# Two small moves in a fused attention and GLU kernel: the loads of the output weights, and the norms of the fourth chunk

## The chip, the cores and the metric

The kernel runs on one core of one Trainium2 chip. A core has five engines with instruction streams of their own: TensorE (PE; matrix products), VectorE (DVE), ScalarE (ACT), GpSimd (POOL), and SyncE (SP), which here issues nearly all DMAs. The metric is device time in microseconds. The kernel before took 311.39 us, the median of three runs (310.5 to 311.7).

## The reference

One transformer block with its two branches side by side, B=1, S=2048 rows, D=640, bf16. Both branches read the same normalised rows.

```python
xn = layernorm(x)                       # over D, eps 1e-5
# A: attention, 32 heads of 20, causal, sliding window of 256 keys
q, k, v = split(xn @ wqkv)              # wqkv: 640 x 1920
p = softmax(where(0 <= i - j < 256, q @ k.T * 20**-0.5, -1e9))
a = (p @ v) @ wo                        # wo: 640 x 640
# B: gated GLU
b = (sigmoid(xn @ w_gate) * (xn @ w_up)) @ w_down   # F = 1536
out = x + a + b
```

## The kernel before, in words

**Chunks.** The 2048 rows are worked in four chunks (c = 0 to 3) of 512 rows, each of four blocks of 128 rows. For each chunk the kernel normalises the rows (`g_norms`), transposes them to `xnT[c]` (for c > 0 by a DMA transpose, `turn_block`), projects Q and K (`g_qk`: five blocks of Q, m = 0 to 4, then five of K, each five matmuls of 128x512), projects V (`g_v`), computes the 12 GLU products (`g_gu`: `pg`, then tanh on ACT, then `pu`, then `h` on DVE, L447), the attention in steps (`scores`, exponentials on ACT at L517, masks on POOL at L524 or as a minimum on DVE at L529, products with V in `pv`, whose sums are `acc`), and last the output (`g_out`: for each block of rows the down projection `y` over 12 `h` at L457, the output projection with `wo` at L464, the addition of x into `rows` at L468, the store at L479).

**Q and K through scratch memory.** A projected block is copied out of PSUM into one of six `st` buffers (Q by DVE at L323, K by ACT at L325) and stored to scratch in DRAM (L327, `sq` and `sk`); `spread` (L337) reads it back in the layout of the heads (`qT`, `kT`). An `st` buffer is free again when its store has landed. The Q gather of a chunk waits for all five Q stores.

**wo.** The rows of `wo` are reordered by `turn_wo` (eight DMAs from DRAM to DRAM, `wo_i`), then loaded into SBUF by `load_wo` (L237, four DMAs of 200 KB, 32 partitions each). In the program all four are issued at once, behind the fourth Q store of chunk 1 (`g_qk`, c = 1, m = 3); they are preceded on the queue by `wo_i`, five loads of `wd` and two stores that clear scratch.

**Order.** The order is written out by hand: each engine runs its instructions in the program's order. The main loop runs over the attention steps; between two steps a `Fill` object pulls dense work (projections, GLU, output) from a list of generators, a fixed amount per step, and each generator yields after a piece of matmuls. `mix(a, b, first, every)` runs generator a and, after its piece number `first` and then after each `every`-th, takes one step of b. So a generator like `g_norms` is a list of small steps, and an extra empty `yield 0` in it moves what follows behind one more piece of a.

**g_norms.** For each of the four row blocks: two `bn_stats` and a `bn_aggr` on DVE, one block per step. Then, after `behind` empty steps, `rstd_blocks` (two POOL instructions, L286 and L287), four empty steps, and the four normalisations `xn` on DVE (L292), one per step. With `turn` each is followed by its DMA transpose on SP (L303); for chunk 3 the transposes come from `g_turns(3)` after the norms. Chunk 3's norms are mixed first into `gu1b` (GLU products 7 to 11 of chunk 1, ten pieces, one norm step after each) and then, for what is left, into `out1`, after its piece 1 and every third piece from there. `out1` is chunk 1's output with the first GLU product of chunk 2 inside.

Of the kernel before, what the change touches and what calls it, by code (L numbers as in the profile page):

```python
# [20 lines left out]
HG = 4  # L21
# [91 lines left out]
def kernel(  # L113
# [11 lines left out]
    nc = tc.nc  # L125
# [30 lines left out]
    def load_x(c):  # L156
        t = xp.tile([P, SBC, D], BF16, name="xc")
        xc[c] = t
        nc.sync.dma_start(out=t, in_=xr[:, c * SBC:(c + 1) * SBC, :])
# [6 lines left out]
    wo = const.tile([P, DC, D], BF16, name="wo")  # L166
# [33 lines left out]
    def load_gu(t, w, k, lo=0, hi=FS):  # L200
        nc.sync.dma_start(out=t[k][:, :, lo:hi],
                          in_=w.rearrange("(c p) f -> p c f", p=P)[:, :, k * FS + lo:k * FS + hi])
# [24 lines left out]
    wo_i = tc.dram_tile([HG, NG * DH, D], BF16, name="wo_i")  # L227
# [4 lines left out]
                nc.sync.dma_start(out=wo_i[i].rearrange("(b a d) n -> a b d n", a=2, d=DH)[a],  # L232
                                  in_=A_wo.rearrange("(a b i d) n -> i a b d n", a=2, i=HG, d=DH)[i, a])

    def load_wo():
        for i in range(HG):
            nc.sync.dma_start(out=wo[32 * i:32 * i + 32, :, :],  # L237
                              in_=wo_i[i].rearrange("(m j) n -> j m n", j=32))


    ident = const.tile([P, P], BF16, name="ident")
# [39 lines left out]
    def ln_block(c, s, mv=None):  # L281
        return ln_mv(ln_half(c, s, 1, ln_half(c, s, 0)), mv)

    def rstd_blocks(mvs):
        rstds = lnp.tile([P, SBC], FP32, name="rstds", bufs=1)
        nc.gpsimd.tensor_scalar(out=rstds, in0=mvs[:, :, 1], scalar1=EPS, scalar2=None, op0=ADD)  # L286
        nc.gpsimd.tensor_tensor(out=rstds, in0=rstds, in1=neghalf, op=POW)  # L287
        return rstds

    def norm_block(c, s, mv, rstd):  # L290
        xn = lnp.tile([P, D], BF16, name="xn")
        nc.vector.tensor_scalar(out=xn, in0=xc[c][:, s, :], scalar1=mv[:, 0:1],  # L292
                                scalar2=rstd[:, 0:1], op0=SUB, op1=MULT)
        xns[c, s] = xn
# [7 lines left out]
    def turn_block(c, s):  # L302
        nc.sync.dma_start(out=xnT[c][:, :, s * P:(s + 1) * P], in_=xns.pop((c, s)), transpose=True)  # L303

    def new_xnT(c):
        xnT[c] = xtp.tile([P, DC, CW], BF16, name="xnT")
# [5 lines left out]
    def proj_block(w, c, m):  # L312


        base = 0 if w == "q" else D
        ps = ps_d.tile([P, CW], FP32, name="pqk", tag="d")
        for d in range(DC):
            wt = wqkv[:, d, base:base + D].rearrange("p (k m) -> p m k", m=DC)
            nc.tensor.matmul(ps, lhsT=wt[:, m, :], rhs=xnT[c][:, d, :],  # L319
                             start=(d == 0), stop=(d == DC - 1))  # L320
        st = stp.tile([P, CW], BF16, name="st")
        if w == "q":
            nc.vector.tensor_copy(out=st, in_=ps)  # L323
        else:
            nc.scalar.copy(out=st, in_=ps)  # L325
        dst = scratch[w, c % 2].rearrange("(h j) s -> h j s", j=32)
        nc.sync.dma_start(out=dst[:, 4 * m:4 * m + 4, :], in_=st)  # L327

    def spread(w, c, g0, g1):

        half, first = divmod(g0, GH)
        if first == 0:
            qk[w, c, half] = (qp if w == "q" else kp).tile([P, GH, CW], BF16, name=w + "T")
        src = scratch[w, c % 2].rearrange("(a b p) s -> b p a s", a=2, p=P)
        for b in range(g0 // 2, g1 // 2):
            o = 2 * b - half * GH
            nc.sync.dma_start(out=qk[w, c, half][:, o:o + 2, :], in_=src[b])  # L337
# [28 lines left out]
    def g_norms(c, turn, behind=0):  # L366


        new_xnT(c)
        mvs = lnp.tile([P, SBC, nc.vector.BN_AGGR_DIM], FP32, name="mvs", bufs=1)  # L370
        for s in range(SBC):
            ln_block(c, s, mvs[:, s, :])
            if s < SBC - 1:
                yield 0
        for _ in range(behind):
            yield 0
        rstds = rstd_blocks(mvs)
        for _ in range(4):
            yield 0
        for s in range(SBC):  # L380
            norm_block(c, s, mvs[:, s, :], rstds[:, s:s + 1])
            yield 0
            if turn:
                turn_block(c, s)

    def g_turns(c):
        for s in range(SBC):
            turn_block(c, s)
            yield 0

    def g_qk(c):
        for w in "qk":
            for m in range(DC):
                proj_block(w, c, m)
                if c == 0 and w == "q" and m == 1:
                    load_x(1)
                if c == 0 and w == "q" and m == 3:
                    load_gu(wu, B_w_up, 0, FS // 2)
                if c == 1 and w == "q" and m == 3:
                    load_wo()  # L400
                if c and w == "k" and m == 1:
                    spread("q", c, 0, GH)
                yield 5 * MM
        if c == 0:
            spread("q", c, 0, 2)
            spread("k", c, 0, 2)
            spread("q", c, 2, 4)
            spread("k", c, 2, 4)
# [19 lines left out]
    def part(w, d, f):  # L428
        k, first = divmod(f * P, FS)
        return w[k][:, d, first:first + P]  # L430

    def g_gu(c, f0, f1):
        for f in range(f0, f1):
            pg = ps_d.tile([P, CW], FP32, name="pg", tag="d")
            for d in range(DC):
                nc.tensor.matmul(pg, lhsT=part(wg, d, f), rhs=xnT[c][:, d, :],  # L436
                                 start=(d == 0), stop=(d == DC - 1))
            th = tp.tile([P, CW], FP32, name="th")
            nc.scalar.activation(out=th, in_=pg, func=TANH, scale=0.5)  # L439
            yield 5 * MM  # L440
            pu = ps_d.tile([P, CW], FP32, name="pu", tag="d")
            for d in range(DC):
                nc.tensor.matmul(pu, lhsT=part(wu, d, f), rhs=xnT[c][:, d, :],  # L443
                                 start=(d == 0), stop=(d == DC - 1))
            h = hp.tile([P, CW], BF16, name="h")
            ht[c, f] = h
            nc.vector.scalar_tensor_tensor(out=h, in0=th, scalar=1.0, in1=pu, op0=ADD, op1=MULT)  # L447
            yield 5 * MM
# [6 lines left out]
    def down(c, s, y, cut):  # L455
        for f in range(FC):
            nc.tensor.matmul(y[:, 0:cut[1] - cut[0]], lhsT=ht[c, f][:, s * P:(s + 1) * P],  # L457
                             rhs=wd[:, f, cut[0]:cut[1]], start=(f == 0), stop=False)
            if f % 6 == 5:
                yield 6 * 136  # L460
# [11 lines left out]
    def new_rows(c, s, name="rows", bufs=3, queue=nc.sync):  # L472
        rows = lnp.tile([P, D], BF16, name=name, bufs=bufs)
        queue.dma_start(out=rows, in_=xr[:, c * SBC + s, :])
        return rows
# [5 lines left out]
    def outp(c, s, ys, rows):  # L481
        for y, cut in zip(ys, HALVES):
            add_wo(c, s, y, cut)
        for y, cut in zip(ys, HALVES):
            add_x(y, cut, rows)
        store(c, s, rows)

    def g_out(c, between, ahead=()):
        nxt = new_rows(c, 0)
        for s in range(SBC):  # L490
            rows = nxt
            if s == 0:
                yield from ahead
            if s + 1 < SBC:
                nxt = new_rows(c, s + 1)
            ys = [ps_d.tile([P, CW], FP32, name=f"y{i}", tag="d") for i in range(2)]
            for y, cut in zip(ys, HALVES):
                yield from down(c, s, y, cut)
            if s == 0:
                yield from between  # L500
            outp(c, s, ys, rows)
            yield 10 * 136
# [115 lines left out]
    def mix(a, b, first, every=1, rest=True):  # L618

        for k, cost in enumerate(a):  # L620
            yield cost
            if k >= first and (k - first) % every == 0:
                yield next(b, 0)
        if rest:
            yield from b
# [70 lines left out]
    for _ in g_qk(0):  # L696
        pass
    load_rest()

    fill = Fill()  # L700
    GU = 10 * MM
    OUT = 4 * 34 * 136
# [5 lines left out]

    norms1 = g_norms(1, True)
    norms2 = g_norms(2, True, 1)  # L710
    norms3 = g_norms(3, False)
    fill.add("gu0a", mix(g_gu(0, 0, 4), norms1, 4, 1, False), 4 * GU)
    fill.add("gu0b", mix(g_gu(0, 4, 12), norms1, 0), 8 * GU)
    fill.add("x2", later(load_x, 2), 0)
# [7 lines left out]
    fill.add("qk2", g_qk(2), 50 * MM)  # L722
    fill.add("v2", mix(g_v(2), g_gu(1, 3, 7), 0, 1), 40 * 136 + 4 * GU)
    fill.add("gu1b", mix(g_gu(1, 7, 12), norms3, 0, 1, False), 5 * GU)
    fill.add("out1", mix(g_out(1, g_gu(2, 0, 1)), itertools.chain(norms3, g_turns(3)), 1, 3), OUT + GU)
    fill.add("qk3", g_qk(3), 50 * MM)
    fill.add("v3", mix(g_v(3), g_gu(2, 1, 5), 0, 1), 40 * 136 + 4 * GU)
    fill.add("gu2", g_gu(2, 5, 12), 7 * GU)
# [39 lines left out]
    c = NCH - 1  # L768
# [62 lines left out]
```

## Time and profile before

| | |
|---|---|
| median of three runs | 311.39 us (310.5, 311.7, 311.39) |
| the profiled execution's own time | 312.31 us |
| its span, first to last instruction | 310.5 us |
| granted TensorE clock | 1.000 |
| DMA moved | 35.67 MB, mean 115 GB/s |
| idle time of TensorE in the body, by the table of waits | 1.4 us on DVE `pT`, 0.8 us on DVE `h` |

The profile is of one execution. Times in it are microseconds from the first instruction. "Idle before" is the time that an engine stood still ahead of an instruction, with what ended it behind an arrow. Matmuls are pipelined: each starts some 0.14 us (128x320) behind the one before, while its printed length is about 0.30 us. SP's rows (SPq) are issues of DMAs, not their transfers; when a transfer has landed is told by the updates of its semaphore in the trace, 16 of them for each DMA.

### The profile page before, as it was taken

The page shows a single profiled execution, that of the slowest core. Times are in us where ns is not written, and L with a number is a line of the kernel's source. Part 1 is how long each engine was busy: PE and PEld are TensorE (multiplying, and loading weights), DVE is VectorE, ACT ScalarE, POOL GpSimd, SP SyncE. Part 2 cuts the span into 40 slices and gives each one's busy share as a digit, 9 for nine tenths or more (in the row PEclk, how much of TensorE's full clock was granted, in tenths as well). Part 3 has the DMA queues.
Part 4 walks back from the last instruction along what each step waited for, and adds up shares of the span by engine and source line. Part 5 has one row for each costly group of instructions (what it writes and reads, how often), then busy time and mean ns, then how long its engine had stood idle before and what let it go on. Part 6 is the DMA issues. An engine that isn't in the chain of part 4 may idle for free.

```text
span 310.5 us, 10034 instructions
## 1 busy us (share of the span) xinstructions
PE 302.4 (97%) x4343; PEld 168.1 (54%) x4343; DVE 172.0 (55%) x342; ACT 198.4 (64%) x196; POOL 165.3 (53%) x304
## 2 busy tenths in 40 slices
PE   6999999998999999999989999999999999999996
PEld 3654444544657654554556665454546665444774
DVE  5633684828697464496945346373643626372533
ACT  6923868668964648888654548978675647778000
POOL 3020668457885828566661836747383756657000
PEclk9999999999999999999999999999999999999999
DMA  7997984985705453440013512640000210000201
GB/s 206 365 327 237 330 155 150 344 260 165 231 0 89 108 158 121 155 160 2 3 23 88 87 56 89 211 155 1 4 0 4 67 40 23 2 2 2 87 23 63
DMA packets 40459, 35.67 MB, mean 115 GB/s; under 512 B 10560, under 2 KB 39872, under 8 KB 40384
## 3 DMA queue, kind: packets, MB, share of 16 engines
q1 hardware_dynamic: 39552, 34.27, 37.2%
q10 hardware_dynamic: 864, 0.77, 0.9%
q8 instruction: 34, 0.56, 0.8%
q14 instruction: 9, 0.07, 0.1%
HBM read 23.63 MB, written 10.26 MB: 109 GB/s over the span
## 4 chain that ended last, share of the span: by engine, by line
PE 90%; DVE 4%; DMA 2%; ACT 2%; issue 1%; SPq 0%; DVEq 0%; ACTq 0%
PE y L457 17%; PE pu L443 17%; PE pg L436 16%; PE pqk L319 12%; PE ps L512 8%; PE pv L349 7%; PE y L464 7%; PE acc L543 6%; DMA sq<-st 1%; ACT pT L517 1%; DVE on L567 1%; DMA xc<-in_A_x_dram 1%; DVE st L323 1%; DVE xn L292 1%; DVE h L447 0%
## 5 line engine op out<-in xcount | busy, mean ns | idle before, releaser
L524 POOL TENSOR_SCALAR_AFFINE_SELECT pT<-pT 64x512 bf16<-64x512 bf16 (+1 forms) x252 | 153.6, 609 | 103.6 <-ACT pT L517 91.8
L517 ACT ACTIVATE pT<-ps 128x2048 bf16<-128x2048 f32 x75 | 140.8, 1877 | 60.4 <-PE ps L512 57.5
L447 DVE SCALAR_TENSOR_TENSOR h<-th,pu 128x512 bf16<-128x512 f32 x48 | 32.8, 683 | 54.3 <-PE pu L443 41.7
L443 PE MATMUL pu<-xnT,wu 128*128 128x512 bf16 x240 | 59.8, 380 | 0.0
L436 PE MATMUL pg<-xnT,wg 128*128 128x512 bf16 x240 | 59.8, 380 | 0.0
L457 PE MATMUL y<-wd,h 128*128 128x320 bf16 (+2 forms) x396 | 56.8, 295 | 0.8 <-DVE h L447 0.8
L319 PE MATMUL pqk<-xnT,wqkv 128*128 128x512 bf16 x200 | 46.0, 381 | 0.0
L457 PEld LDWEIGHTS <-h 128*128 128x128 bf16 x396 | 36.6, 98 | 17.0 <-issue 2.2
L439 ACT ACTIVATE th<-pg 128x512 f32<-128x512 f32 x48 | 28.6, 596 | 15.3 <-PE pg L436 15.1
L436 PEld LDWEIGHTS <-wg 128*128 128x128 bf16 x240 | 22.3, 98 | 25.6 <-issue 2.0
L443 PEld LDWEIGHTS <-wu 128*128 128x128 bf16 x240 | 22.1, 98 | 25.4 <-issue 1.8
L319 PEld LDWEIGHTS <-wqkv 128*128 128x128 bf16 x200 | 22.6, 119 | 18.8 <-issue 1.4
L512 PE MATMUL ps<-qT,kT 20*64 20x320 bf16 (+4 forms) x1456 | 32.2, 259 | 0.3 <-issue 0.2
L512 PEld LDWEIGHTS <-kT 20*64 20x64 bf16 x1456 | 15.9, 103 | 24.8 <-issue 21.8
L555 DVE STREAM_TRANSPOSE t<-acc 128x512 f32<-128x512 f32 x32 | 21.1, 696 | 13.3 <-PE acc L543 13.3
L567 DVE TENSOR_TENSOR on<-t,rec 128x320 bf16<-128x320 f32 (+4 forms) x48 | 27.7, 576 | 1.1
L468 DVE SCALAR_TENSOR_TENSOR rows<-y,rows 128x320 bf16<-128x320 f32 x30 | 14.4, 488 | 23.8 <-PE y L464 23.5
L349 PE MATMUL pv<-wqkv,xnT 128*128 128x320 bf16 x160 | 25.9, 300 | 0.0
L464 PE MATMUL y<-wo,oc 128*128 128x320 bf16 (+2 forms) x165 | 24.2, 295 | 0.0
L543 PE MATMUL acc<-pT,v 64*32 64x320 bf16 (+4 forms) x1456 | 19.8, 252 | 1.4 <-DVE pT L529 1.4
L358 DVE CAST v<-pv 64x320 bf16<-64x320 f32 x29 | 14.1, 487 | 12.2 <-PE pv L349 11.9
L543 PEld LDWEIGHTS <-v 64*32 64x32 bf16 x1456 | 16.3, 91 | 7.4 <-issue 2.6
(48 smaller groups left out, 157.3 us busy)
## 6 DMA issues: line engine op xcount, KB each, us to landing
qT<-sq SPq DMA_DIRECT2D x16, 256.0 KB
kT<-sk SPq DMA_DIRECT2D x16, 256.0 KB
sq<-st SPq DMA_DIRECT2D x20, 128.0 KB
sk<-st SPq DMA_DIRECT2D x20, 128.0 KB
out_dram<-rows SPq DMA_DIRECT2D x15, 160.0 KB
wg<-in_B_w_gate_dram SPq DMA_DIRECT2D x4, 480.0 KB
wu<-in_B_w_up_dram SPq DMA_DIRECT2D x4, 480.0 KB
xc<-in_A_x_dram SPq DMA_DIRECT2D x3, 640.0 KB
```

The costliest lines, as they stand in the source:

```text
L319: nc.tensor.matmul(ps, lhsT=wt[:, m, :], rhs=xnT[c][:, d, :], start=(d == 0), stop=(d == DC - 1))
L349: nc.tensor.matmul(ps[:, 0:HALF], lhsT=xnT[c][:, d, s * P:(s + 1) * P], rhs=wqkv[:, d, 2 * D + hf * HALF:2 * D + (hf + 1) * HALF], start=( ...
L436: nc.tensor.matmul(pg, lhsT=part(wg, d, f), rhs=xnT[c][:, d, :], start=(d == 0), stop=(d == DC - 1))
L443: nc.tensor.matmul(pu, lhsT=part(wu, d, f), rhs=xnT[c][:, d, :], start=(d == 0), stop=(d == DC - 1))
L447: nc.vector.scalar_tensor_tensor(out=h, in0=th, scalar=1.0, in1=pu, op0=ADD, op1=MULT)
L457: nc.tensor.matmul(y[:, 0:cut[1] - cut[0]], lhsT=ht[c, f][:, s * P:(s + 1) * P], rhs=wd[:, f, cut[0]:cut[1]], start=(f == 0), stop=False)
L464: nc.tensor.matmul(y[:, 0:cut[1] - cut[0]], lhsT=oc[c, m][:, s * P:(s + 1) * P], rhs=wo[:, m, cut[0]:cut[1]], start=False, stop=(m == DC - 1))
L512: nc.tensor.matmul(ps[a * U:(a + 1) * U, i, col * U:(col + n) * U], lhsT=qk["k", kc, o // GH][32 * i:32 * i + DH, o % GH + a, kb * U:(kb + ...
L517: nc.scalar.activation(out=pt[:, :, 0:CW], in_=ps, func=EXP, scale=SCALE)
L524: nc.gpsimd.affine_select(out=view, in_=view, pattern=[[0, HG], [0, n], [sign, U]], compare_op=GE, fill=0.0, base=base, channel_multiplier ...
L543: nc.tensor.matmul(acc[32 * i:32 * i + 32, q * U:(q + n) * U], lhsT=vt[kb][a * U:(a + 1) * U, u, h * VW:h * VW + 32], rhs=pt[a * U:(a + 1) ...
L567: nc.vector.tensor_tensor(out=on[m][:, :, slot:slot + n], in0=t1[:, :, first:first + n], in1=rec.to_broadcast([P, 16, n]), op=MULT)
```

## The change

Two edits. First, `load_wo` takes an index and issues one load; `g_qk` of chunk 1 calls it behind each of the Q stores m = 0, 1, 2 and 3 instead of four times behind m = 3. Second, chunk 3's norms get two empty steps between the statistics and `rstd_blocks`, and their rest is taken in `out1` after every second piece instead of every third.

```diff
-    def load_wo():
-        for i in range(HG):
-            nc.sync.dma_start(out=wo[32 * i:32 * i + 32, :, :],
-                              in_=wo_i[i].rearrange("(m j) n -> j m n", j=32))
+    def load_wo(i):
+        nc.sync.dma_start(out=wo[32 * i:32 * i + 32, :, :],
+                          in_=wo_i[i].rearrange("(m j) n -> j m n", j=32))
...
-                if c == 1 and w == "q" and m == 3:
-                    load_wo()
+                if c == 1 and w == "q" and m < HG:
+                    load_wo(m)
...
-    norms3 = g_norms(3, False)
+    norms3 = g_norms(3, False, 2)
...
-    fill.add("out1", mix(g_out(1, g_gu(2, 0, 1)), itertools.chain(norms3, g_turns(3)), 1, 3), OUT + GU)
+    fill.add("out1", mix(g_out(1, g_gu(2, 0, 1)), itertools.chain(norms3, g_turns(3)), 1, 2), OUT + GU)
```

HG is 4. On DVE the order around the last GLU product of chunk 1 changes from h, xn, xn, h, xn, xn, h to h, h, xn, xn, xn, h, xn. On POOL the two `rstds` instructions move behind the next four mask instructions. On SP the order of the stores q0 to q4 and the loads w0 to w3 changes from q0 q1 q2 q3 w0 w1 w2 w3 q4 to q0 w0 q1 w1 q2 w2 q3 w3 q4, and the four transposes T of chunk 3 stand among the output stores S and row loads R as S R T T S T R T S S instead of T S R T T S R T S S. TensorE's and ACT's orders stay.

## The prediction

> **What bounds the kernel now.** I read the page's busy shares first, then the chain of waits over the whole span, then the timeline around the two places where that chain leaves TensorE, then the DMA semaphore updates in the trace.
>
> ```profile
> PE 302.4 (97%) x4343; PEld 168.1 (54%) x4343; DVE 172.0 (55%) x342; ACT 198.4 (64%) x196; POOL 165.3 (53%) x304
> ```
>
> TensorE has work for 302.4 of 310.5 us, at a granted clock of 1.000. So 8.1 us are idle, and most of it is the start and the tail. The table of waits has only two TensorE entries in the body: `acc` behind DVE `pT` (1.44 us, at 70.87) and `y` behind DVE `h` (0.84 us, at 157.53). The chain is TensorE's nearly throughout; it leaves for other engines at 58.6 to 70.9 and at 150.0 to 157.5. The two parts of the change fall into exactly these stretches: part one issues its DMAs at 60 to 67, part two moves vector work of 155 to 158.
>
> The first stretch, from the timeline of 54 to 75 us (start, length, engine, line; in brackets the idle time before and what ended it):
>
> ```profile
> 60.02 4.18 SPq L327 DMA_DIRECT2D sq<-st  x4
> 64.25 2.78 SPq L237 DMA_DIRECT2D wo<-wo_i  x4
> 67.12 0.52 SPq L327 DMA_DIRECT2D sq<-st  x1
> 67.18 1.07 ACT L325 CAST st<-pqk 128x512 bf16<-128x512 f32 x2 [2.04 <-DMA sq<-st]
> 68.14 1.90 ACT L517 ACTIVATE pT<-ps 128x2048 bf16<-128x2048 f32 x1
> 70.14 0.68 DVE L529 TENSOR_TENSOR pT<-pT,edge 128x512 bf16<-128x512 bf16 x1 [5.89 <-ACT pT L517]
> 70.87 0.36 PE L543 MATMUL acc<-pT,v 64*32 64x64 bf16 x24 [1.44 <-DVE pT L529]
> ```
>
> Read it backwards. TensorE waits for a mask (DVE), which waits for an exponential (ACT), which stands on ACT behind two copies of K blocks, k1 and k2. k1 waited 2.04 us for a free `st` buffer (six of them): it reuses Q store q0's, k2 reuses q1's. So the landings of q0 and q1 set the end here.
>
> The second stretch, from the timeline of 146 to 172 us:
>
> ```profile
> 154.72 0.65 DVE L447 SCALAR_TENSOR_TENSOR h<-th,pu 128x512 bf16<-128x512 f32 x1
> 155.03 1.67 PE L457 MATMUL y<-wd,h 128*128 128x320 bf16 x11
> 155.29 1.59 DVE L292 TENSOR_SCALAR xn<-xc,mvs,rstds 128x640 bf16<-128x640 bf16 x2
> 156.81 0.67 DVE L447 SCALAR_TENSOR_TENSOR h<-th,pu 128x512 bf16<-128x512 f32 x1
> 157.40 0.94 DVE L292 TENSOR_SCALAR xn<-xc,mvs,rstds 128x640 bf16<-128x640 bf16 x2
> 157.53 1.94 PE L457 MATMUL y<-wd,h 128*128 128x320 bf16 x13 [0.84 <-DVE h L447]
> ...
> 162.30 0.69 DVE L447 SCALAR_TENSOR_TENSOR h<-th,pu 128x512 bf16<-128x512 f32 x1 [3.96 <-ACT th L439]
> 164.88 2.54 SPq L303 DMA_TRANSPOSE xnT<-xn  x2
> ```
>
> The down projection consumes GLU products 0 to 10 and stops for product 11: its `h` stands on DVE behind two `xn` of chunk 3 that nobody needs before 181 us.
>
> **Part one, the `wo` loads.** Nothing is added or removed; three Q stores go behind one, two and three loads, and the fifth stays behind all four. SP keeps eight DMAs in flight: each issue waits for the landing of the eighth before it. The semaphore updates show it (last update, next issue): first `wd` load 61.10, q1 61.17; clear of the Q scratch 65.78, third `wo` load 65.80; clear of the K scratch 66.70, fourth 66.72; q0 67.02, q4 67.12. These landings do not depend on the change, so the issues of after follow: q0 60.02, wo0 61.2, q1 62.4, wo1 63.3, q2 64.1, wo2 64.9, q3 65.8, wo3 66.7, q4 67.1. Before, q1, q2 and q3 went at 61.17, 62.41 and 63.68; q4 does not gain.
>
> Landings lag issues by 7 us (q0: 60.02 to 67.02) because four of the sixteen DMA engines are behind: of each landing's 16 updates four come late (clear of Q: twelve by 62.94, the last at 65.78). Packets of 25,600 B, the `wo_i` turns, take some 960 ns each until 58 us, one after another on few engines. On the slowest engine the landings come in the order of issue: q0 67.02, q1 67.35, q2 67.67, q3 68.11, wo0 68.95, wo1 69.77, wo2 70.56, wo3 71.02, q4 71.31. A store takes 0.33 there, a load 0.46 to 0.84. With wo0 between q0 and q1, q1 lands at 67.02 + 0.84 + 0.33 = 68.19; with k1's lag of 0.16 (67.02 to 67.18) k2 starts at 68.35 instead of 67.66: +0.69. With the cheapest load (0.46) it is 67.97: +0.31. I take +0.6, by the nearest row, wo0's own, a little less since wo0 has longer to be fetched ahead. Nothing can be gained: k1 still waits for q0. From below the bound is 0 (wo0's bytes moved while the engine is idle), from above 2.5, should the load's full time from issue to first landing (wo0: 64.25 to 66.71) stand in the queue. Exponential, mask and the masked `acc` pieces follow k2 one to one, and TensorE is already waiting there, so the 0.6 is lost whole (part of it shows earlier, at 68.6: the first `acc` pieces take a bank that k2's copy frees). k3 and k4 wait for q2 (69.34) and q3 (70.6), due at 70.5 and 71.0 by then: covered. The Q gather waits for q4, which lands last in both orders, near 71.3; its first reader is at 79.9, and the pieces land by 78.5.
>
> The Trainium skill (DMA: Bandwidth & Descriptors, Anatomy of one DMA) gives about 2.0 us fixed plus bytes over 436e3 per microsecond, fitted on GpSimd's path: an estimate of 0.47 us of movement for a load of 204,800 B. By that, q1 lands at 67.82, part one costs 0.32 and the whole sum is -0.68; the 0.79 to 0.84 of the first three loads speak for more, the 0.46 of the fourth for it.
>
> **Part two, the norms of chunk 3.** The two extra empty steps put `rstds` on POOL behind four selects, and the `xn` on DVE behind the last `h`. The instruction order of the changed kernel gives on DVE h10, h11, xn, xn, xn, h(next chunk), xn; TensorE's and ACT's orders stay. h11's product is ready (pu of 153.50 ends 154.74), so h11 runs at 155.3 to 156.0. The eleventh `y` matmul starts at 156.40; at 0.136 apart the twelfth is due at 156.53. It started at 157.53. So the gain is 1.00 us, more than the 0.84 printed, since printed ends overlap the next start. From below: 0.84; if h11 were as late as 0.5 us more it would still be in time.
>
> What is late next: (a) POOL. `rstds` (0.23 + 1.04) stood in idle time at 148.64; now it follows the selects that end at 153.71, done by 155.1; the next four selects end near 158.0 instead of 156.70, the four after them near 160.5 instead of 159.60, and then POOL idled until 161.84 (now 160.84). Their reader is the `acc` at 166.28. Covered. (b) DVE. Three `xn` of 0.44 to 0.93 from 156.0 end by 158.8; the next `h` is due at 161.3: covered by the 3.96 us of idle time. The fourth `xn` now stands before the two `rows` additions, which start 0.5 later than they would; the next `y` takes the buffer of `pg`, freed by ACT, and only the `acc` needs theirs, 1.5 us later. (c) SP. The first transpose moves from 156.24 to behind the first output store (164.01), the third behind the second (170.79), ahead of a row load. A transpose holds SP 1.2 to 2.4 us. The last is issued at most 2.8 later than 171.65 and lands at most by 178.7 (before: 175.88); chunk 3's first projection reads it at 181.34, or 180.3 with the gain. The store of 176.52 may find SP busy for 0.3 us; nothing waits for it. Covered; it costs only past 1.6 us more.
>
> **Sum.** -1.00 + 0.60 = -0.4 us. The profiled execution took 312.31 (span 310.5 and 1.8 around it), so it would be 311.9; the median of the runs shown is 311.39, which gives **311.0**.
>
> **Rivals.** (1) The load costs q1 nothing, since its bytes move in gaps: only part two counts, -1.0, 310.4. For it: the DMA engines are busy 0.80 and 0.70 of the windows 62 to 64 and 64 to 66 us. Against: the slowest engine, which decides, is in arrears until 71. (2) Slower: part one's wait is dearer. If the slow engine serves a `wo` load whole before the next store, reading back `wo_i` with its full 2.5 us, k2 comes 2.5 late: +1.5 net, 312.9. It beats part two from 1.0 on. For it: 4.7 us from wo0's issue to its last update. Against: successive loads came 0.8 apart. (3) Part two gains nothing: `rstds` so late on POOL that the `xn` block the next `h`, which feeds nothing for 2 us but frees a `y` buffer. It needs `rstds` after 158.5; I work out 155.1. Then +0.6, 312.0.
>
> **Numbers.** Forecast 0.55, rival one 0.2, two 0.13, three 0.12. Bounds of the forecast alone: -1.0 + 0.3 to -0.84 + 0.7, 310.7 to 311.25. The range takes in rivals one and three and the spread of the runs (310.5 to 311.7): 310.0 to 312.3. What a measurement of this kernel can tell from no change is about 0.5%, 1.6 us; no case but the far end of rival two reaches it, nor does the whole gain without loss. So faster 0.04, same 0.88, slower 0.08.
>
> **What would show it.** Right: no TensorE wait for `h` near 156; four transposes issued after 163; TensorE's waits between 68.5 and 71.5 us grown from 1.44 to about 2.0 in all, with k2's copy apart from k1's. Wrong: k2 straight behind k1 (rival one); waits there over 2.4 (rival two); a DVE wait for `rstds` or a TensorE wait near 181.

## The result, and the profile after

The changed kernel took 313.68 us, the median of 7 runs (312.39 to 314.04), beside 311.59 us (310.5 to 312.1, 7 runs) for the kernel before on the same chip: a ratio of 1.0062, 95% interval 1.0039 to 1.0084. It is slower by some 2 us where 0.4 us less was forecast, and outside the range on record. The profiled execution took 313.68 us; its span is 311.9.

The first page of the changed kernel's profile, the line of busy time and the granted TensorE clock in 40 slices (tenths of full speed):

```profile
PE 301.6 (97%) x4308; PEld 168.9 (54%) x4343; DVE 172.4 (55%) x342; ACT 198.6 (64%) x196; POOL 165.2 (53%) x304
...
PEclk9999999997999999999999999999999999999999
```

Busy time is as before. New is one digit: a 7 in the tenth slice (70 to 78 us). The mean clock of this execution is 0.994; before it was 1.000. Line numbers in the changed kernel are lower by one.

The timeline of the changed kernel, 54 to 75 us:

```profile
60.28 0.35 SPq L236 DMA_DIRECT2D wo<-wo_i  x1
...
61.54 0.52 SPq L326 DMA_DIRECT2D sq<-st  x1
...
67.33 0.59 ACT L324 CAST st<-pqk 128x512 bf16<-128x512 f32 x1 [1.92 <-DMA sq<-st]
67.99 1.18 SPq L326 DMA_DIRECT2D sk<-st  x2
68.35 0.59 ACT L324 CAST st<-pqk 128x512 bf16<-128x512 f32 x1 [0.43 <-DMA sq<-st]
...
68.86 0.97 PE L542 MATMUL acc<-pT,v 64*32 64x320 bf16 x56
...
71.55 0.36 PE L542 MATMUL acc<-pT,v 64*32 64x64 bf16 x24 [1.72 <-DVE pT L528]
...
72.20 2.54 PE L348 MATMUL pv<-wqkv,xnT 128*128 128x320 bf16 x10
```

The load w0 now stands between the stores q0 and q1, and the copies k1 and k2, which ran back to back before, are 0.43 us apart: k2 waits for q1. TensorE's wait for the mask is 1.72 us instead of 1.44. All this was foreseen, with a wait of about 2.0. The last row was not: ten `pv` matmuls take 2.54 us. Before, with the clock at 1.000, they took 1.53:

```profile
71.52 1.53 PE L349 MATMUL pv<-wqkv,xnT 128*128 128x320 bf16 x10
```

The table of windows says why. Its columns are the stretch, its length, busy time of PE, PEld, DVE, ACT and POOL with their instructions in brackets, then the granted clock, the DMA share and GB/s. Changed kernel:

```profile
65.73:69.15 3.42, 3.37 (x64) 1.74 (x71) 0.00 (x0) 1.39 (x3) 1.57 (x3) 1.00 0.77 239
69.15:72.56 3.41, 1.69 (x99) 1.04 (x80) 1.25 (x2) 2.67 (x4) 1.63 (x4) 1.00 0.42 126
72.56:75.97 3.41, 3.19 (x12) 1.69 (x12) 3.19 (x7) 2.58 (x3) 2.70 (x6) 0.50 0.72 250
75.97:79.38 3.41, 3.41 (x50) 1.73 (x55) 2.13 (x6) 2.82 (x3) 1.46 (x5) 1.00 0.70 202
```

From 72.56 us TensorE is granted half its clock, for 3.41 us. In the 3.41 us ahead of that it was busy for 1.69, a little under half. The kernel before, in the stretch of the same length that holds its wait, was busy for 1.97 and kept its clock:

```profile
68.47:71.88 3.41, 1.97 (x100) 1.24 (x100) 1.25 (x2) 2.67 (x4) 1.63 (x4) 1.00 0.63 177
71.88:75.29 3.41, 3.41 (x45) 2.03 (x44) 3.33 (x8) 3.35 (x5) 2.70 (x6) 1.00 0.81 259
```

The second place, timeline of the changed kernel, 146 to 172 us:

```profile
157.09 1.25 DVE L446 SCALAR_TENSOR_TENSOR h<-th,pu 128x512 bf16<-128x512 f32 x2
...
157.39 3.43 PE L456 MATMUL y<-wd,h 128*128 128x320 bf16 x24
...
158.26 2.31 DVE L291 TENSOR_SCALAR xn<-xc,mvs,rstds 128x640 bf16<-128x640 bf16 x3
```

The two `h` now run one behind the other, the 24 `y` matmuls form one row with no wait in it, and the `xn` follow.

Both kernels load weights into TensorE in the same order (4,373 loads), so each load's start can be set against its partner's. In times of the trace of before, the changed kernel's trace minus that of before: +0.28 us until 68.5 (the start of the kernel, which the change does not touch), +0.68 at 70.87, +2.36 from 79.8 to 140, +1.35 at 157.6 and 165, +1.37 at the end. So in this execution the stall costs 0.40, the halved clock 1.68, and part two gives back 1.01.

### The profile page after: what moved, and what is told of

The parts are those of the page before. It is cut to its first block, busy times and chain, and to the rows that moved or that the text cites. A ratio compares the mean times of both kernels' runs of the same rounds, so it can differ in the third digit from the quotient of the medians.

```text
span 311.9 us, 10000 instructions
## 1 busy us (share of the span) xinstructions
PE 301.6 (97%) x4308; PEld 168.9 (54%) x4343; DVE 172.4 (55%) x342; ACT 198.6 (64%) x196; POOL 165.2 (53%) x304
## 4 chain that ended last, share of the span: by engine, by line
PE 88%; DMA 5%; DVE 2%; issue 2%; ACT 2%; SPq 1%; ACTq 0%; DVEq 0%
PE y L456 17%; PE pg L435 16%; PE pu L442 16%; PE pqk L318 11%; PE ps L511 8%; PE pv L348 8%; PE y L463 7%; PE acc L542 5%; DMA sq<-st 2%; DMA wqkv<-in_A_wqkv_dram 2%; DMA xc<-in_A_x_dram 1%; ACT pT L516 1%; DVE st L322 0%; SPq L176 0%; DVE pT L528 0%
## 5 line engine op out<-in xcount | busy, mean ns | idle before, releaser
L435 PE MATMUL pg<-xnT,wg 128*128 128x512 bf16 x225 | 59.0, 382 | 1.3 <-issue 0.5
L442 PE MATMUL pu<-xnT,wu 128*128 128x512 bf16 x230 | 58.9, 380 | 0.7 <-issue 0.3
L318 PE MATMUL pqk<-xnT,wqkv 128*128 128x512 bf16 x190 | 45.1, 381 | 0.8 <-issue 0.4
L348 PE MATMUL pv<-wqkv,xnT 128*128 128x320 bf16 x160 | 26.9, 308 | 0.2 <-DMA wqkv<-in_A_wqkv_dram 0.2
```

The lines of the kernel that those rows point to most:

```text
L348: nc.tensor.matmul(ps[:, 0:HALF], lhsT=xnT[c][:, d, s * P:(s + 1) * P], rhs=wqkv[:, d, 2 * D + hf * HALF:2 * D + (hf + 1) * HALF], start=( ...
```

## The experiments

Three causes were to be told apart: the longer wait makes the clock halve in part of the executions; the wait for q1 costs time by itself; and, as came up later, q0 lands later as well when the loads are spread. The texts on record letter their theories for each run anew, so A is not the same theory in all of them. Where "the trace" of a run is compared with that of before, both are set against each other load by load, as above.

**Each part alone.** `p1_only` is the changed kernel with the two lines of `norms3` and `out1` as before; `p2_only` is the kernel before with those two lines changed.

> Part one alone (loads of wo spread, norms as before). Theory A: the second Q store lands behind the first wo load, the K copy k2 starts some 0.4 us later against k1, TensorE's stall at 69 to 71 us grows by 0.4 us, and the longer stall makes the clock halve for 3.4 us in most executions: 0.4 more without the halving, 2.0 more with it, median 313.0 to 313.8 against 311.6. Rival B (the halving in the profile of after came by chance and has nothing to do with the stall): granted clock 1.000 as before, about 312.0.

> Part two alone (norms moved, loads of wo as before). Theory A: TensorE's wait for h near 157 us is gone, 1.05 us less, nothing else moves, clock 1.000: 310.5. Rival (part two brings a wait of its own, behind the transposes or rstds, that the profile of after hides): 311.3 or more, with a TensorE wait near 162 or 181 us.

Part one alone: 314.09 us (312.01 to 315.04, 7 runs) beside 311.95, ratio 1.006 [1.0023, 1.0098]. Part two alone: 310.76 (309.92 to 312.85, 12 runs), 0.9972 [0.9954, 0.999]. The clock was halved in 3 of 7 executions of the first and in none of 12 of the second. Against the trace of before, `p2_only` goes from -0.14 us at 140 to -1.16 at 157.6: a gain of 1.02. So part one alone shows the whole loss, and part two alone its gain. By the medians the two do not add up: +2.1 and -1.2 us alone, +2.1 together. The interval of `p1_only` (0.7 to 3.1 us) is wide enough to hold that.

**The loads one store later.** `pair_first`: norms as before, loads behind q1, q2, q3 and q3, so that q0 and q1 stay neighbours.

```diff
-                if c == 1 and w == "q" and m == 3:
-                    load_wo()
+                if c == 1 and w == "q" and 0 < m < HG:
+                    load_wo(m - 1)
+                if c == 1 and w == "q" and m == 3:
+                    load_wo(3)
```

> Part one changed in one thing: the first two Q stores go together, the four loads stand behind the second, third, fourth and fourth Q store; norms as before. Theory A (only the landing of the second Q store matters): k2 follows k1 at once, stall 1.4 us as before, clock 1.000, 311.6. Rival C (spreading the loads costs in itself, through the later stores): k3 and k4 or the Q gather late, 312.0 or more.

312.34 us beside 311.95, 1.0011 [0.9991, 1.0032], no clock halved in 12. Its k1 and k2 are back to back, its stall 1.36. Spreading loads is nearly free; what costs is the one between q0 and q1.

**A longer wait without the change.** `before_st5` is the kernel before with five `st` buffers instead of six.

> The kernel before with five st buffers instead of six; no load of wo is moved. The K copies then wait for Q stores q0, q1, q2 instead of free, q0, q1; worked out from the landings 67.02, 67.35, 67.67 the exponential starts 0.5 us later and TensorE stalls 0.4 to 0.5 us longer. Theory A (the clock follows the length of the stall, whatever causes it): the clock halves in a part or most of the executions, 312.1 without it and up to 313.7 with it. Rival D (the halving belongs to the moved loads, not to the stall): clock 1.000 in all executions, 312.1.

312.78 us, 1.0031 [1.0015, 1.0047], no halved clock in 12. The premise failed in the trace: q0 landed at 66.51, 0.94 us earlier than before against TensorE's work, and the stall was 0.98 us, shorter than before. TensorE was only 0.45 us earlier, so the missing buffer did cost the 0.5 that was expected; but with so short a stall the run settles nothing about the clock.

`act_copy1` and `act_copy2` are the kernel before with one or two more ACT copies (of a constant into a spare tile, work that the kernel doesn't need) between k2's copy and the exponential:

```diff
+                if c == 1 and w == "k" and m == 2:
+                    for _ in range(1):
+                        nc.scalar.copy(out=idle, in_=ones)
```

> The kernel before with one extra 128x512 copy on ACT (a constant into an unused tile) between the K copy k2 of chunk 1 and the exponential behind it; all DMAs as before. The exponential, the mask and the masked products start 0.5 to 0.6 us later, so TensorE's stall at 69 to 71 us grows to about 2.0 us as in the changed kernel. Theory A (the clock follows the stall, whatever causes it): the clock is halved for 3.4 us in about half of the executions (granted clock 0.995 instead of 1.000); 0.5 more without it, 2.1 more with it. Rival D (the halving belongs to the moved loads of wo): clock 1.000 in all executions, 0.5 more.

> The same with two such copies: the stall grows to about 2.5 us. Theory A: the clock halves in nearly all executions, 1.0 + 1.6 = 2.6 us more than before. Rival D: clock 1.000, 1.0 more. Rival E (the halving is a matter of chance, alike for all kernels): the same share of halved executions as with one copy.

One copy: 312.2 us beside 311.76, 1.0017 [0.9996, 1.0037], the clock halved in 1 of 12. The forecast was half of them. In its trace q0 landed at 66.00, 1.09 us earlier than before against TensorE's work, and the stall was only 0.85 instead of 2.0. Two copies: 312.79, 1.0037 [1.0014, 1.0059], halved in 3 of 12, where nearly all were forecast and 2.6 us instead of the 1.0 measured. The traced execution was one of the three. The table of windows of `act_copy2`:

```profile
70.55:73.96 3.41, 1.41 (x46) 0.90 (x46) 1.65 (x3) 2.69 (x4) 1.99 (x5) 1.00 0.32 76
73.96:77.37 3.41, 3.41 (x11) 1.24 (x9) 3.33 (x8) 2.16 (x3) 2.72 (x6) 0.50 0.69 239
```

A stall of 2.70 us, no load moved, and the same 3.41 us at half clock, which cost 1.68 us. So the clock can halve behind a long wait with no load moved: the idle time is enough. The counts alone (1 and 3 of 12) are too few to tell one copy from two.

**The stall taken away.** `after_st8` and `p2_st8` have eight `st` buffers, so that k1 and k2 wait for no store.

```diff
-    stp = pool("stp", 6)
+    stp = pool("stp", 8)
```

> The changed kernel with eight st buffers instead of six, so that the K copies k1 and k2 wait for no store; the loads of wo stay spread. Theory A: the stall at 69 to 71 us is gone, clock 1.000, and the spread loads cost nothing: before less 1.05 (norms) less 1.4 (stall), about 309.5. Rival D (the loads cost in themselves): still slower than the kernel before or with the clock at 0.995.

> Part two with eight st buffers and the loads of wo as in the kernel before. Theory A: as the changed kernel with eight buffers within 0.3 us, about 309.5, so that the place of the loads does not matter once no copy waits. Rival: apart from it by 0.5 us or more, then the loads cost on another way.

`after_st8`: 311.23 us (11 runs), 0.999 [0.9974, 1.0007], halved in 1 of 11. `p2_st8`: 311.36 (12), 1.0001 [0.9985, 1.0016], halved in none. Without the wait for q1 the loss is gone, but so is most of the gain that was expected: at 70.87 both are 1.6 to 1.7 us ahead of the kernel before, and at 79.8 they are 0.3 and 1.0 behind. The timeline of `p2_st8`:

```profile
70.38 1.52 PE L349 MATMUL pv<-wqkv,xnT 128*128 128x320 bf16 x10 [0.48 <-DVE t L555]
...
80.86 0.43 PE L512 MATMUL ps<-qT,kT 20*64 20x320 bf16 x24 [1.51 <-DMA kT<-sk]
```

TensorE waits for DVE first and then for the gather of K. That gather's last of 16 updates came at 80.82; the other fifteen had come by 78.52. A wait removed at 70 us met the next one at 79.

**The turns of wo over all DMA engines.** The prediction traced the late landings to the `wo_i` turns, whose packets run on few engines. `wo16_before` and `wo16_after` are the two kernels with the same bytes cut into sixteen parts:

```diff
-                nc.sync.dma_start(out=wo_i[i].rearrange("(b a d) n -> a b d n", a=2, d=DH)[a],
-                                  in_=A_wo.rearrange("(a b i d) n -> i a b d n", a=2, i=HG, d=DH)[i, a])
+                dst = wo_i[i].rearrange("(b a d) n -> a b (d n)", a=2, d=DH)[a]
+                src = A_wo.rearrange("(a b i d) n -> i a b (d n)", a=2, i=HG, d=DH)[i, a]
+                nc.sync.dma_start(out=dst.rearrange("b (e m) -> e b m", e=16),
+                                  in_=src.rearrange("b (e m) -> e b m", e=16))
```

> The changed kernel with the eight wo_i turns cut into 16 pieces of 1,600 B rows each instead of 4 of 25,600 B, so that they run on all DMA engines. Theory A (the stall comes from the arrears of the few DMA engines that carry wo_i, and the moved loads lengthen it there alone): Q stores land some 2.5 us after their issue, no K copy waits, the stall at 69 to 71 us and the halved clock are gone, and the K gather lands before its reader: before less 1.05 (norms) less 1.0 to 1.6 (stall), 309.0 to 309.8. Rival F (the arrears come from the sheer bytes of wd, wo_i and the clears on all engines): q0 still lands past 66 us and the time stays above 311.

> The kernel before with the same spread turns. Theory A: no stall either, 310.2 to 310.9, and the changed kernel with spread turns is faster than this one by the 1.05 us of the norms alone, so the place of the wo loads costs nothing once no engine is in arrears. Rival F: 311.6 as before.

`wo16_after`: **309.96 us** (309.34 to 310.18, 6 runs) beside 311.37, 0.9948 [0.9927, 0.9968], no clock halved; it beats both kernels. `wo16_before`: 311.62 (12 runs, one with the clock halved), 1.0004 [0.9982, 1.0025], a miss. The timeline of `wo16_before`:

```profile
66.36 0.52 SPq L329 DMA_DIRECT2D sq<-st  x1
...
68.60 1.04 PE L545 MATMUL acc<-pT,v 64*32 64x320 bf16 x80
...
78.95 0.43 PE L514 MATMUL ps<-qT,kT 20*64 20x320 bf16 x24 [0.61 <-ACT v L360]
```

The stall at 70 is gone (80 `acc` in one row, -1.60 us), but only 0.91 is left at 79.8. The last row names ACT as what ended its wait, but the K gather's last update came at 78.90, just ahead of it. In `wo16_after` the fifth Q store is issued at 65.02 instead of 66.36 and has landed by 67.95 instead of 70.41, and the K gathers go 1.7 to 2.5 us earlier; of its 1.53 us at 70.87 nothing is lost by 79.8, and part two adds 1.01. So in this pair, with the queue not in arrears, the loads between the stores do good. At the end of the traces `wo16_before` stands 1.7 us behind `wo16_after`; 1.0 of it is part two's.

**Two executions more.** `after_again` and `p1_again` are the changed kernel and part one alone again, one traced execution each, in the hope of one at full clock.

> The changed kernel once more, for the trace of a second execution: where the clock is not halved (granted 0.999 or 1.000), its executions took 312.4 to 313.0, 1.3 more than the 311.0 to 311.3 that 0.4 to 0.8 of stall and 1.05 of gain give. Theory A: the stall in such an execution is longer than in the first trace (2.5 us or more, between two windows of the clock). Rival G: the K gather lands late, TensorE waits near 80 us.

> Part one alone once more, for the trace of a second execution; its executions without a halved clock took 312.0 to 315.0. Theory A: the stall at 69 to 72 us differs between executions with the landing of the first Q store (66 to 68 us in the traces so far) and is 1 us or more longer than in the kernel before. Rival G: TensorE waits near 80 us for the K gather.

312.98 us and 314.56; the clock was halved in both, at 71.36 and 73.15 us, for 3.41 us each time, so neither shows the changed kernel at full clock.

**One load alone, and two more executions.** `w0_first` and `w0_third` are the kernel before with only w0 moved, behind q0 or behind q2; w1 to w3 stay behind q3. `after_l3` is the changed kernel, `p1_l3` part one alone, one traced execution each.

```diff
-                if c == 1 and w == "q" and m == 3:
-                    load_wo()
+                if c == 1 and w == "q" and m == 0:
+                    load_wo(0)
+                if c == 1 and w == "q" and m == 3:
+                    load_wo(1), load_wo(2), load_wo(3)
```

(In `w0_third` the first condition is m == 2.)

> The kernel before with one edit: only the load wo0 is issued early, behind q0; wo1 to wo3 stay behind q3. Theory A (a load issued at 60.3 us delays the fourth wd load, and with it q0, and the load itself stands between q0 and q1): from the third to the fourth wd load (last landings) 1.5 to 1.95 us, q0 8.2 to 9.2 us behind the end of wo_i, q1 0.9 to 1.2 behind q0, q2 again 0.33 behind q1; the time as with part one alone, 312.6 to 314 us, with halved clocks in some executions. Theory B (the later q0 comes from several loads in the queue, or was chance): wd gap 0.8 to 0.85, q0 7.2 to 7.8 behind wo_i's end, q1 0.9 to 1.2 behind q0; the time +0.3 to +0.7 us over the kernel before. Theory C (one load costs q1 nothing): gap of q1 0.33, no difference in time.

> The kernel before with one edit: wo0 is issued behind the third Q store (q2, some 64.5 us), wo1 to wo3 stay behind q3. Both A and B expect q0 7.2 to 7.8 us behind the end of wo_i, q1 and q2 0.33 apart behind it, q3 some 0.9 behind q2, which only k4's copy waits for, and that is covered: the time is the kernel before's within 0.3 us, with hardly a halved clock. If one load anywhere in the queue delays q0 (against A and B), q0 comes 8.2 to 9.2 behind and the time grows by about 1 us.

> The changed kernel again, one look, for an execution whose clock is not halved. With the load between q0 and q1 alone: TensorE's wait near 70 us some 0.6 to 0.7 longer than before and a time near 311.2. With a later q0 as well: some 1.5 longer, a time near 312. If the clock is halved again: 313.5 to 314, and the question stays open.

> Part one alone again, one look, for an execution whose clock is not halved. With the load between q0 and q1 alone: TensorE 0.6 to 0.7 us behind the kernel before from 71 us on, a time near 312.2. With a later q0 as well: some 1.5 behind, near 313. If the clock is halved again: 314 to 314.6.

`w0_first`: 314.16 us (312.74 to 315.15, 8 runs) beside 312.13, 1.0069 [1.0043, 1.0095], halved in 4 of 8. `w0_third`: 311.82 (12 runs), 1.0011 [0.999, 1.0031], halved in 2 of 12. One load behind q0 costs as much as the whole of part one; the same load two stores later costs nothing that can be measured. The traced execution of `w0_first` (314.03, full clock) lost 0.60 us near 70 and 0.78 more near 207, where the score products `ps` start after 0.94 us of idle time (0.16 before). `pair_first` and `p1_again` have such a wait there too, 0.82 and 0.72 us; what ends it the profile does not tell. The timelines, first of `w0_first`:

```profile
67.75 0.58 ACT L324 CAST st<-pqk 128x512 bf16<-128x512 f32 x1 [2.25 <-DMA sq<-st]
68.62 0.58 ACT L324 CAST st<-pqk 128x512 bf16<-128x512 f32 x1 [0.28 <-DMA sq<-st]
...
71.82 0.36 PE L544 MATMUL acc<-pT,v 64*32 64x64 bf16 x24 [1.72 <-DVE pT L530]
```

and of `w0_third`:

```profile
67.86 1.07 ACT L324 CAST st<-pqk 128x512 bf16<-128x512 f32 x2 [1.43 <-PE ps L513]
...
71.55 0.36 PE L544 MATMUL acc<-pT,v 64*32 64x64 bf16 x24 [0.83 <-DVE pT L530]
```

Copies apart and 1.72 us of waiting in the one, copies together and 0.83 in the other. Of the forecasts of theory A for `w0_first` one missed clearly: the last gap between the landings of `wd` loads (the third and the fourth, counted from 0) was 0.74 us, not 1.5 to 1.95. Two missed narrowly: q1 came 0.87 us behind q0 (0.9 to 1.2), and the time was 314.16 (312.6 to 314).

`p1_l3` took 313.0 us at a full clock, the execution that was missing. From 70.87 us to 165 it stands 0.71 to 0.72 us behind the trace of before: 0.5 from q1's place behind w0, 0.2 because q0 itself lands 0.22 later than in that trace. Its table of windows:

```profile
67.53:70.94 3.41, 2.20 (x62) 1.05 (x60) 0.10 (x1) 3.00 (x4) 0.13 (x1) 1.00 0.74 236
70.94:74.36 3.42, 2.78 (x54) 1.71 (x54) 2.92 (x6) 2.66 (x4) 2.69 (x6) 1.00 0.63 211
```

It has the same wait of 1.72 us as the changed kernel, but the wait lies across a border of the windows, 1.21 on one side and 0.64 on the other (small pauses included), and the clock stays whole. `after_l3` took 315.57: q0 landed at 68.43, TensorE lost 1.95 us by 70.87, and the clock was halved twice over, from 71.79 for 6.83 us:

```profile
68.38:71.79 3.41, 1.38 (x58) 0.69 (x57) 0.00 (x0) 2.80 (x3) 0.00 (x0) 1.00 0.77 248
71.79:75.21 3.42, 2.44 (x46) 1.22 (x46) 2.00 (x3) 2.30 (x4) 2.83 (x6) 0.50 0.51 133
75.21:78.62 3.41, 3.41 (x11) 1.27 (x9) 3.14 (x8) 1.54 (x3) 2.44 (x5) 0.50 0.45 150
```

## Why the prediction was wrong

**The issues and the gap of q1: right.** Issues came within some 0.9 us of those worked out (w0 60.28, q1 61.54, q2 63.58, q3 65.97, q4 67.24). q1 landed 0.87 to 1.02 us behind q0 in the seven traces with w0 behind q0 and six buffers, where 1.17 was worked out, and 0.32 before. k2 started at 68.35, the time worked out, but by luck: 0.28 of that is this execution's later start. TensorE lost 0.40 us there in the profiled execution, 0.60 in `w0_first` and 0.71 in `p1_l3`, which holds the movement of q0 as well. Before, k2 started 0.64 behind q0's landing; now it starts 0.16 behind q1's. So the gap alone costs 0.96 + 0.16 - 0.64 = 0.5 in the mean, against the 0.6 of the sum. That and q0's own movement against the trace of before give TensorE's loss at 70.87 within 0.02 us in each of the seven traces. Rival one (no cost) falls with these; rival two's mechanism (the store waits for a load's full 2.5 us) falls with the gap of 1.0, though its time, 312.9, was the nearest. k3, k4 and the Q gather were covered, as said (q3's landing comes to 70.46 by the rows used, not 70.6; nothing hangs on it).

**Part two: right.** -1.01 us here and -1.02 in `p2_only`, against -1.00; rival three falls. The margins of POOL, of the fourth `xn` and of the transposes held: no wait for `rstds`, and from 165 to 200 us, over chunk 3's first projections, the changed kernel loses nothing (+1.35, then +1.14).

**What failed first: the clock was left out.** The sum took TensorE's clock as 1.000 throughout, because the page of before shows it. It did not ask what a longer wait does to it. The granted clock answers in steps. In the six traces in which it was halved here, the distance from that drop to the one in the tail is a whole multiple of 3.4133 us: 238.93 us in four of them, 70.00 times, and 242.35 in two, 71.00 times. So the clock seems to be set at the borders of windows of this length, which in each execution can be drawn from any drop, and TensorE's idle time be read in the window around 70 us that has most of it:

| Execution | idle in the fullest window, us | next window |
|---|---|---|
| `w0_third`, `act_copy1`, `before_st5` | 0.83, 0.85, 0.98 | full clock |
| `w0_first`, `p1_l3` (the wait lies across a border) | 1.11, 1.21 | full clock |
| `p2_only`, `pair_first`, before | 1.29, 1.36, 1.44 | full clock |
| changed kernel, `after_again`, `p1_again` | 1.72, 1.72, 1.72 | half clock |
| `p1_only`, `act_copy2`, `after_l3` | 1.90, 2.00, 2.03 | half clock |

The limit lies between 1.44 and 1.72 us of idle time here, and the kernel before stood within 0.3 us of it. Elsewhere in these traces windows with up to 1.57 us keep the clock and those with 2.20 or more lose it, but two at the end of the kernel keep it with 1.75 (`p1_only`, 307.5 us) and 1.77 us (`p1_l3`, 306.5). The ends of matmuls are modelled in a trace, so the limit may be blurred by that. Half a window, 1.707 us, lies near it; that it is the limit is not shown. With w0 behind q0 the wait for `pT` is 1.72 us in all seven such traces with six buffers, enough if it falls whole into one window. It does so for (3.41 - 1.72) / 3.41 = 50% of the possible positions; the clock was halved in 14 of the 26 executions of the changed kernel, `p1_only`, `w0_first` and the four single executions, and in 3 of 101 of the kernel before that ran beside the experiments. A halved window cost 1.5 to 1.7 us from 70.87 to 79.8 in the five traces that have one, so half of the executions make some 0.8 us in the mean. The Trainium skill (TensorE: Matmul & The Clock Gate, Part 1) states a free-running window of 3,413 ns and a clock that is either whole or half; these traces agree, with 3.41 us and 0.50. It has the clock halved after an idle window, and warns of gaps over some 3.4 us; here 1.72 us within one window was enough.

**What failed second: "These landings do not depend on the change".** In the eight traces with w0 behind q0 and the old turns, q0's last landing, set to the same TensorE instruction ahead of it, lies at 66.9 to 68.5 us, mean 67.5; in the eight traces with no load there, at 65.9 to 67.1, mean 66.6. That is 0.85 us later in the mean (0.5 between the medians). Set against the end of the `wo_i` turns in the same trace, the two sets part: 8.2 to 9.2 us with w0 behind q0, 7.2 to 7.8 without, and 8.2 in `pair_first`, whose w0 is issued one store later, at 61.61. The place is the `wd` loads: from the last landing of the first to that of the fifth pass 5.0 to 5.5 us with w0 behind q0, 4.9 in `pair_first`, 3.7 to 4.4 in the others. The single trace of before hid this: its q0, at 67.02, is among its latest, and its execution (312.31) among the slower ones. The forecast corrected for that with the median, but kept q0 of that trace. The times at full clock bear it out: `p1_only` and `w0_first` average 313.35 and 313.37 us there (four executions each, 312.01 to 315.04), 1.3 and 1.4 over the mean of the kernel before on their chips, where q1's gap alone gives 0.5. That a load issued at 60 us takes the slow engines' time ahead of older transfers, the `wd` loads that land until 65, is my reading; no run shows how.

**The sum, as measured:** part two -1.0; q1 behind w0 +0.5; q0 later +0.85 in the mean; the clock +0.8 in the mean. Together some +1.15 us, of 2.1 between the medians (interval 1.2 to 2.6). The median execution of the changed kernel is itself a halved one, for which the terms give some +1.95. But its three executions at full clock, 312.39 to 312.98, lie 0.8 us on average over 311.59 - 1.0 + 0.5 + 0.85. That rest is not settled; the wait near 207 us, which differs by up to 0.8 us from trace to trace, may hold part of it.

## What to carry to other kernels

Before a wait of TensorE is made longer, or one is left as harmless, put its length beside the idle time that halves the clock: here some 1.7 us within one window of 3.41 us, where 0.3 us more of waiting cost another 1.5 to 1.7 in about every second execution. A transfer that TensorE waits for, at a few steps' distance, should have nothing new issued between it and its older neighbours while the queue is in arrears; look first for what causes the arrears, since here that fix (`wo16_after`) turned the same change from a loss into a gain. And one trace of before is one sample: where a landing decides, take its spread from several.

## What the runs showed of the hardware

- A clock that has been halved seems to be given back under another condition than the one that keeps it, by a single case: `after_l3` was busy for 2.44 of the 3.42 us of its first half-clock window (71%) and stayed at half clock for a second one; the changed kernel was busy for 3.19 (93%) and got the full clock back. At full clock windows with a busy share as low as that 71% kept it (`before_st5`, 0.98 us idle).
- In `p2_st8` one of the 16 updates of a K gather came late, at 80.82, 2.3 us after the fifteenth, beside a packet of the instruction queue (16,384 B, at 78.2 us). It was seen once and not tried by itself, so that the one delayed the other is not shown.
- Single executions at a clock of 1.000 are 1.5 to 2 us over the median without any change (four of 30 of the kernel before on one chip, 313.5 to 313.9). None was traced; why stays open.
